# Hedgehog attention and a gated MLP on one core: the first loads change queues, and their order changes

## The chip, the cores and the metric

The kernel runs on one core of one Trainium2 chip. The core has five engines with instruction queues of their own: PE (TensorE, matrix multiplication and transposes, results in PSUM), DVE (VectorE), ACT (ScalarE), POOL (GpSimd) and SP (SyncE, which here only issues transfers). Transfers between main memory and the on-chip memory are moved by 16 DMA engines. A transfer issued by SP or ACT goes through what the profile calls a hardware queue (q1 for SP, q10 for ACT), one issued by POOL through a software queue (q0). In this kernel the transfers that change the number type on the way, fp32 in memory to bf16 on the chip, are issued by POOL; those that SP issues keep the type.

The metric is the device time of one execution in microseconds. The kernel before the change took 287.19 us (median of 11 runs, 286.33 to 287.76).

## The reference

Two layers follow each other. The first is linear attention with learned features (8 batches, 8 heads, 576 tokens, 64 values a head, 128 features; all in fp32):

```python
def phi(x):
    proj = einsum('bhsd,df->bhsf', x, w_phi)
    proj = proj - max(abs(proj), axis=-1, keepdims=True)
    return concatenate([exp(proj), exp(-proj)], axis=-1)
q_p, k_p = phi(q), phi(k)
kv  = einsum('bhsf,bhsd->bhfd', k_p, v)
z   = sum(k_p, axis=2)
num = einsum('bhsf,bhfd->bhsd', q_p, kv)
den = einsum('bhsf,bhf->bhs', q_p, z)[..., None] + 1e-06
return num / den
```

The second takes the result as x, 8 batches of 576 tokens by 512:

```python
h = maximum(x @ w_in, 0.0)                 # w_in 512 x 1024
u, v = h[..., :512], h[..., 512:]
v_n = (v - mean(v)) / sqrt(var(v) + 1e-06) # over the last axis
v_s = einsum('ts,bsd->btd', w_spatial, v_n) + b_spatial[None, :, None]
return (u * v_s) @ w_out
```

What matters here: the sums kv and z of a head run over all 576 tokens of it, so no output of a head can be formed before all its keys and values were seen.

## The kernel before, in words

**Tiles.** 576 tokens are four blocks of 128 and a tail of 64. Two heads of one batch, four blocks each, make one *pair unit*: 128 partitions (tokens) and eight slots (two heads by four blocks). The tails of all eight heads of two batches make one *tail unit*: 64 + 64 partitions and eight slots, one a head. Two batches make a group g; its tail unit is shared by its eight pair units, since each head's sum needs its tail tokens too. The units are worked through in the order: unit 0 and 1 (batch 0, heads 0 to 3), unit 2 (the tail of batches 0 and 1, the "shared tail"), units 3 and 4 (batch 0, heads 4 to 7), units 5 to 8 (batch 1), unit 9 (the tail of batches 2 and 3), and so on: 36 units.

**What a unit does.** `a_transpose` (lines 243 to 256) turns k and q on PE, and DVE (at first) copies them out. `a_keys` multiplies by `w_phi`, DVE takes the maxima of the absolute values (line 273), ACT the two exponentials kf of the key features (line 276). `a_scale` (lines 293 to 309) lets ACT form em, exp of minus and plus the maximum (line 296), and then POOL multiplies v by em: vs for a pair unit (lines 301 and 303), vst for a tail unit (`tail_scale`, lines 311 to 318). So the keys' maximum is not subtracted, but multiplied into v. `a_queries` and `a_max_t` find and turn the queries' maxima (POOL makes mhl from unit 5 on, lines 290 and 291), `a_qfeat` forms the query features qf. `a_kv` (lines 363 to 379) sums kv on PE: for each head and sign four matrix products over the blocks (line 373) and one over the tail's rows (line 375), into one PSUM bank. Every pair unit of a batch therefore waits for that batch's half of vst. `a_num` multiplies by qf and divides.

**The second layer.** When a batch's four pair units are through, its matrix products go into a list of tasks (`b_tasks`), from which the steps fill PE. POOL normalises v there (vn, line 459) and makes the means and roots (lines 451 to 455).

**Steps.** The main loop runs steps i = 0, 1, ...; in step i come the keys of unit i with their scaling, its queries, the transposes of unit i + 1, and the later stages of earlier units, with lags. After step i the transfers of `io[i]` are issued, as the lines `at(i, ...)` at the end of the kernel say (lines 675 to 707): loads of later batches, weights, and for batch 0 and 1 some filling.

**Order on an engine.** The framework orders instructions of an engine by its own simulation, but what is wrapped in `pin` (line 60) stays behind everything already written for its engine. All loads are pinned, and so are fills, casts of the head and `tail_scale`. An engine works its queue in order: while POOL waits for a transfer, what stands behind it waits too, the transfers that it would issue among them.

**The head.** SP loads the first two k and q quarters of batch 0 as fp32 (`first`), which are then cast, two by DVE and two by POOL (lines 162 and 179). POOL issues the rest in this order (lines 174 to 184): the tails of k and q (two loads each, one a batch), k and q of heads 4 and 5, the first half of v; then its two casts; the tail of v (two loads), k and q of heads 6 and 7, the second half of v. The constants `vnt`, rows of the identity that carry the spatial bias through the tail's product, are filled by ACT for even groups before the steps and by POOL for odd ones after step 1 (`fill_vnt`, line 165). The buffers `v_f` for v exist twice; `k_tl`, `q_tl` and `v_tl` for the tails once.

Of the kernel before, what the change touches and what calls it, by code (L numbers as in the profile page):

```python
# [8 lines left out]
FP32 = mybir.dt.float32  # L9
# [7 lines left out]
def kernel(  # L17
# [15 lines left out]
    nc = tc.nc  # L33

    B, H, S, D = q.shape
    F = w_phi.shape[1]
    DM = moe_w_in.shape[0]
    DFF = moe_w_in.shape[1]
    HALF = DFF // 2
    P = 128  # L40
    KC = DM // P
    NP = H // 2
    NB = 4
    T0 = NB * P
    TL = S - T0
# [5 lines left out]
    ld = ctx.enter_context(tc.tile_pool(name="loads", bufs=2))  # L51
# [8 lines left out]
    def pin(start):  # L60
        return lambda *a, **kw: tc.keep_in_program_order(start(*a, **kw))  # L61

    def main_ap(t, b, h0=0, n=H):
        return bass.AP(tensor=t.tensor, offset=t.offset + (b * H + h0) * S * D,
                       ap=[[NB * D, P], [S * D, n], [1, NB * D]])

    def tail_ap(t, b):
        return bass.AP(tensor=t.tensor, offset=t.offset + b * H * S * D + T0 * D,
                       ap=[[D, TL], [S * D, H], [1, D]])

    st = {}
    gs = {}

    XB = 2

    def alloc(b):
        st[b] = dict(
            q=[None, None], k=[None, None],
            v=ld.tile([P, H * NB, D], FP32, tag="v_f", name="v_f"),
        )  # L80

    def alloc_tail(g):
        gs[g] = dict(
            q=ld.tile([P, H, D], BF16, tag="q_tl", name="q_tl", bufs=1),
            k=ld.tile([P, H, D], BF16, tag="k_tl", name="k_tl", bufs=1),
            v=ld.tile([P, H, D], FP32, tag="v_tl", name="v_tl", bufs=1),
        )

    def half_tile(x, b, y):
        if b not in st:  # L90
            alloc(b)
        if st[b][x][y] is None:
            n = f"{x}_bf{(2 * b + y) % 4}"
            st[b][x][y] = ld.tile([P, 4, NB * D], BF16, tag=n, name=n, bufs=1)
        return st[b][x][y]

    def load(x, b, y, h0=0, n=4):
        t = half_tile(x, b, y)
        pin(nc.gpsimd.dma_start)(out=t[:, h0:h0 + n], in_=main_ap(q if x == "q" else k, b, 4 * y + h0, n))

    def load_v(b, y=None, eng=nc.sync):
        if b not in st:
            alloc(b)
        h0, n = (0, H) if y is None else (4 * y, 4)
        pin(eng.dma_start)(
            out=st[b]["v"][:, h0 * NB:(h0 + n) * NB, :].rearrange("p (h c) d -> p h (c d)", h=n),
            in_=main_ap(v, b, h0, n))

    def load_tail(x, g, veng=nc.sync):
        if g not in gs:  # L110
            alloc_tail(g)
        t, eng = dict(q=(q, nc.gpsimd), k=(k, nc.gpsimd), v=(v, veng))[x]
        for i in range(2):
            pin(eng.dma_start)(out=gs[g][x][i * TL:(i + 1) * TL], in_=tail_ap(t, 2 * g + i))
# [12 lines left out]
    first = {}  # L127
    for h0 in (0, 2):
        for x, t in (("k", k), ("q", q)):
            first[x, h0] = s2.tile([P, 2, NB * D], FP32, tag="ob", name="first", bufs=6)  # L130
            pin(nc.sync.dma_start)(out=first[x, h0], in_=main_ap(t, 0, h0, 2))
    ident = cpool.tile([P, P], BF16)
    make_identity(nc, ident)
    zero = cpool.tile([P, 1], BF16)
# [11 lines left out]
    for i in range(NM):  # L146
        for tiles, name in ((mhl, "mhl"), (mT, "mT")):
            t = cpool.tile([P, P], BF16, name=f"{name}{i}")
# [16 lines left out]
    def fill_vnt(i, copy):  # L165
        for bl, row in ((0, TL), (1, 0)):
            pin(copy)(out=vnt[i][:, bl, :], in_=ident[:, row:row + 1].to_broadcast([P, HALF]))

    pin(nc.scalar.copy)(out=vst[0].rearrange("p b s h d -> p (b s h d)"), in_=zero.to_broadcast([P, 4 * H * DA]))
    for y in range(2):  # L170
        r = slice(y * D, (y + 1) * D)
        pin(nc.scalar.copy)(out=wphi2[r, y * F:(y + 1) * F], in_=wphi_f[r, :])
    fill_vnt(0, nc.scalar.copy)
    load_tail("k", 0)
    load_tail("q", 0)
    load("k", 0, 1, 0, 2)
    load("q", 0, 1, 0, 2)
    load_v(0, 0, nc.gpsimd)
    for x in ("k", "q"):
        pin(nc.gpsimd.tensor_copy)(out=half_tile(x, 0, 0)[:, 2:4], in_=first[x, 2])  # L180
    load_tail("v", 0, nc.gpsimd)
    load("k", 0, 1, 2, 2)
    load("q", 0, 1, 2, 2)
    load_v(0, 1, nc.gpsimd)

    w_in_bf = cpool.tile([P, KC, DFF], BF16)
    w_out_bf = cpool.tile([P, KC, DM], BF16)
    wsp = s2.tile([P, NB, T0], BF16, tag="vn", name="wsp", bufs=2)
    wspr = cpool.tile([P, NB, TL], BF16)
# [5 lines left out]
    rows = moe_w_spatial[0:T0, :].rearrange("(p c) s -> p c s", c=NB)  # L195
    cols = moe_w_in.rearrange("(kc p) f -> p kc f", p=P)
# [472 lines left out]
    AT, AB, XP = 5, 6, 3  # L669
    io = {}  # L670

    def at(i, f, *a):
        io.setdefault(i, []).append(lambda: f(*a))

    at(0, load, "k", 1, 0)
    at(0, load, "q", 1, 0)
    at(1, fill_vnt, 1, nc.gpsimd.tensor_copy)
    at(1, load, "k", 1, 1)
    at(1, load, "q", 1, 1)
    at(1, load_v, 1)  # L680
    at(2, load_weight, w_in_bf[:, :, HALF:DFF], cols[:, :, HALF:DFF])
    at(4, load_weight, wsp, rows[:, :, 0:T0])
    at(4, load_weight, wspr, rows[:, :, T0:S])
    at(4, load_weight, wspt, moe_w_spatial[T0:S, :])
    at(5, tail_scale, 0, 1)
    at(5, load_weight, w_in_bf[:, :, 0:HALF], cols[:, :, 0:HALF])
    at(8, load_weight, w_out_bf, moe_w_out.rearrange("(kc p) f -> p kc f", p=P))
    for u in units:
        i = u["i"]
        if not u["pair"] and u["g"] > 0:  # L690
            early = 1 if u["g"] > 1 else 0
            at(i - AT - early, load_tail, "k", u["g"])
            for x in ("q", "v"):
                at(i - AT + 1 - early, load_tail, x, u["g"])
        if u["pair"] and u["b"] >= XB:
            if u["pj"] == 0:
                for n, (x, y) in enumerate((("k", 0), ("q", 0), ("k", 1), ("q", 1))):
                    at((3, 3, 5, 6)[n] if u["b"] == XB else i - AB + n, load, x, u["b"], y)
                for y in range(2):
                    at(i - AB + 1 + 2 * y, load_v, u["b"], y)  # L700
            for x in ("k", "q"):
                at(i - XP, cross, x, u)
# [41 lines left out]
```

## Time and profile before

| | |
|---|---|
| median of 11 runs | 287.19 us |
| the profiled execution, whole | 287.0 us |
| its span, first to last instruction | 285.0 us |
| mean granted clock of PE | 0.985 |
| PE busy | 258.6 us, 91% |
| DVE busy | 230.3 us, 81% |
| ACT busy | 220.5 us, 77% |
| POOL busy | 203.6 us, 71% |
| read from main memory, written | 32.85 MB, 9.44 MB |

Times in the profile are counted from the span's start. A row of the timeline gives start, duration, engine, line, operation, the tile written and the tile read, and in brackets how long the engine had been idle before it and what released it. A row of the waits gives who waited for whom, the sum, how often, and the longest. The chain is followed back from the last instruction, at each step to what released it; a DMA in it begins when it was issued. Line 61 is the pin helper, so pinned instructions all carry that line and are told apart by their tiles. A transfer "lands" when its semaphore says so; its piece counts are those of the written side. Issuing a transfer takes POOL 0.5 to 0.9 us, which its rows show as work of its own; on SP it is a row of SPq.

### The profile page before, as it was taken

The page shows a single profiled execution, that of the slowest core. Times are in us where ns is not written, and L with a number is a line of the kernel's source. Part 1 is how long each engine was busy: PE and PEld are TensorE (multiplying, and loading weights), DVE is VectorE, ACT ScalarE, POOL GpSimd, SP SyncE. Part 2 cuts the span into 40 slices and gives each one's busy share as a digit, 9 for nine tenths or more (in the row PEclk, how much of TensorE's full clock was granted, in tenths as well). Part 3 has the DMA queues.
Part 4 walks back from the last instruction along what each step waited for, and adds up shares of the span by engine and source line. Part 5 has one row for each costly group of instructions (what it writes and reads, how often), then busy time and mean ns, then how long its engine had stood idle before and what let it go on. Part 6 is the DMA issues. An engine that isn't in the chain of part 4 may idle for free.

```text
span 285.0 us, 8175 instructions
## 1 busy us (share of the span) xinstructions
PE 258.6 (91%) x3042; PEld 172.4 (60%) x3042; DVE 230.3 (81%) x576; ACT 220.5 (77%) x501; POOL 203.6 (71%) x366
## 2 busy tenths in 40 slices
PE   3751988989899899999999999999999999999993
PEld 2531876666666576667666676666765765654441
DVE  6970998986799997998889989997889897566441
ACT  6690898997699997899889987899789977723601
POOL 8679999999987895699958984789558832420710
PEclk9996899999999999999999999999999999999998
DMA  9989999999967999989997999999756301120205
GB/s 188 285 143 132 149 115 134 218 157 205 179 96 125 157 226 199 160 221 194 191 127 109 243 235 145 207 192 229 96 120 132 80 8 44 68 76 37 112 3 184
DMA packets 83420, 42.17 MB, mean 148 GB/s; under 512 B 51122, under 2 KB 78450, under 8 KB 83380
## 3 DMA queue, kind: packets, MB, share of 16 engines
q1 hardware_dynamic: 55796, 29.12, 51.5%
q0 software_dynamic: 27424, 12.46, 36.8%
q8 instruction: 24, 0.39, 0.6%
q14 instruction: 16, 0.13, 0.2%
q10 hardware_dynamic: 160, 0.07, 0.1%
HBM read 32.85 MB, written 9.44 MB: 148 GB/s over the span
## 4 chain that ended last, share of the span: by engine, by line
PE 59%; POOL 20%; DVE 6%; DMA 5%; ACT 4%; issue 3%; POOLq 0%; ACTq 0%; DVEq 0%
PE ps L518 9%; PE pv L442 9%; PE po L543 9%; PE ps L261 6%; PE pu L497 6%; POOL vs L301 5%; PE pv L373 4%; DMA v_f<-in_v_dram 4%; PE pn L393 4%; POOL vst L61 3%; PE pq L339 3%; PE ps L519 2%; ACT kf L276 2%; POOL vn L459 2%; DVE stats L445 2%
## 5 line engine op out<-in xcount | busy, mean ns | idle before, releaser
L276 ACT ACTIVATE kf<-ps 128x512 bf16<-128x512 f32 x144 | 76.2, 636 | 8.3 <-DVE mk L273 8.0
L301 POOL TENSOR_TENSOR vs<-v_f,em 128x512 bf16<-128x512 f32 x64 | 65.4, 1041 | 19.6 <-ACT em L296 18.0
L360 ACT ACTIVATE qf<-pq 128x512 bf16<-128x512 f32 x128 | 66.8, 622 | 15.6 <-PE pq L339 8.5
L273 DVE TENSOR_REDUCE mk<-ps 128x4 f32<-128x512 f32 x72 | 47.6, 677 | 0.8
L287 DVE TENSOR_REDUCE mq<-ps 128x4 f32<-128x512 f32 x62 | 39.8, 681 | 2.5 <-PE ps L261 2.2
L518 PE MATMUL ps<-w_spT,vn 128*128 128x512 bf16 x128 | 33.7, 379 | 1.4 <-POOL vn L459 1.4
L521 DVE TENSOR_TENSOR uT<-ps,uT 128x512 bf16<-128x512 f32 x32 | 22.0, 687 | 14.4 <-PE ps L519 14.3
L445 DVE BATCH_NORM_STATS2 stats<-vr 128x6 f32<-128x512 bf16 (+1 forms) x40 | 26.7, 683 | 7.5 <-ACT vr L444 7.1
L543 PE MATMUL po<-w_out_bf,uT 128*128 128x512 bf16 x128 | 32.4, 379 | 0.0
L497 PE MATMUL pu<-xT,w_in_bf 128*128 128x512 bf16 x128 | 32.1, 379 | 0.0
L442 PE MATMUL pv<-w_in_bf,xT 128*128 128x512 bf16 x128 | 31.5, 379 | 0.1
L444 ACT ACTIVATE vr<-pv 128x512 bf16<-128x512 f32 (+1 forms) x40 | 23.5, 616 | 7.3 <-PE pv L442 5.9
L373 PEld LDWEIGHTS <-kf 128*128 128x128 bf16 x512 | 22.1, 98 | 11.3 <-issue 10.3
L375 PE MATMUL pv<-vst,kf 128*128 128x66 bf16 x128 | 21.5, 193 | 7.0 <-POOL vst L61 7.0
L373 PE MATMUL pv<-vs,kf 128*128 128x66 bf16 x512 | 24.8, 195 | 2.9 <-POOL vs L303 1.6
L384 DVE TENSOR_TENSOR x<-pn,rc 128x256 bf16<-128x256 f32 x64 | 24.9, 418 | 0.3
L459 POOL TENSOR_SCALAR vn<-vr,rs 128x512 bf16<-128x512 bf16 x32 | 24.3, 766 | 1.1
L393 PEld LDWEIGHTS <-qf 128*128 128x128 bf16 x512 | 20.4, 98 | 6.8 <-issue 0.8
L499 ACT ACTIVATE uT<-pu 128x512 bf16<-128x512 f32 x32 | 19.7, 641 | 4.9 <-PE pu L497 3.2
L546 ACT COPY ob<-po 128x512 f32<-128x512 f32 x18 | 11.0, 613 | 15.1 <-PE po L543 8.6
L393 PE MATMUL pn<-kv,qf 128*128 128x66 bf16 x512 | 21.9, 194 | 0.3 <-ACT qf L360 0.3
L61 POOL TENSOR_TENSOR vst<-v_tl,em 64x512 bf16<-64x512 f32 x16 | 16.4, 1040 | 5.3 <-ACT em L296 4.9
(134 smaller groups left out, 569.7 us busy)
## 6 DMA issues: line engine op xcount, KB each, us to landing
out_dram<-ob SPq DMA_DIRECT2D x32, 256.0 KB, 2.6
v_f<-in_v_dram SPq DMA_DIRECT2D x12, 512.0 KB, 7.1
k_bf<-in_k_dram POOLq DMA_DIRECT2D x14, 256.0 KB, 5.4
q_bf<-in_q_dram POOLq DMA_DIRECT2D x14, 256.0 KB, 5.2
qt<-qT_b SPq DMA_DIRECT2D x24, 64.0 KB, 4.8
v_f<-in_v_dram SPq DMA_DIRECT2D x1, 1024.0 KB, 8.8
v_f<-in_v_dram POOLq DMA_DIRECT2D x2, 512.0 KB, 8.9
w_in_bf<-in_moe_w_in_dram POOLq DMA_DIRECT2D x2, 512.0 KB, 6.4
```

The costliest lines, as they stand in the source:

```text
L273: nc.vector.tensor_reduce(out=u["mk"][:, hs], in_=pk, axis=AX.X, op=ALU.max, apply_absolute_value=True)
L276: nc.scalar.activation(out=u["kf"][:, s, hs, :], in_=pk, func=AF.Exp, bias=0.0, scale=sc)
L287: nc.vector.tensor_reduce(out=mq[:, 4 * half:4 * half + 4], in_=pq, axis=AX.X, op=ALU.max, apply_absolute_value=True)
L301: nc.gpsimd.tensor_tensor(out=vs[:, s, :, 0:D], in0=st[u["b"]]["v"][:, pj * H:(pj + 1) * H, :], in1=em[:, s, :].unsqueeze(2).to_broadcast( ...
L360: nc.scalar.activation(out=qf[:, s], in_=pq, func=AF.Exp, bias=0.0, scale=sc)
L373: nc.tensor.matmul(out=pv[:, hh, s, :], lhsT=u["kf"][:, s, 4 * hh + c, :], rhs=u["vs"][:, s, 4 * hh + c, :], start=(c == 0), stop=False)
L393: nc.tensor.matmul(out=pn[:, pos, :], lhsT=u["qf"][hh][:, s, pos, :], rhs=d["kv"][:, 2 * u["pj"] + hh, s, :], start=(s == 0), stop=(s == 1))
L442: nc.tensor.matmul(out=pv[r], lhsT=lhs(kc), rhs=w_in_bf[:, kc, HALF:DFF], start=(kc == 0), stop=(kc == KC - 1))
L445: nc.vector.bn_stats(out=stats[r], in_=dst[r])
L497: nc.tensor.matmul(out=pu, lhsT=w_in_bf[:, kc, dc * P:(dc + 1) * P], rhs=d["xT"][:, kc, :], start=(kc == 0), stop=(kc == KC - 1))
L518: nc.tensor.matmul(out=ps, lhsT=d["vn"][:, sp, cs], rhs=w_spT[:, sp, 0:T0], start=(sp == 0), stop=False)
L543: nc.tensor.matmul(out=po[r], lhsT=lhs(dc), rhs=w_out_bf[:, dc, :], start=(dc == 0), stop=(dc == KC - 1))
```

## The change

The first tails, fp32, and batch 0's v come through SP's queue, after the four `first` loads and in this order: tail of k (two loads), tail of q (two), first half of v, tail of v (two), second half of v. The k and q tails land in a buffer `tails` of the kind of `v_f`, and POOL casts them to `k_tl` and `q_tl`. All four `vnt` fills are made by POOL ahead of its other work; the ones of ACT and the later ones of POOL are gone. POOL's two casts of `first` then come before its loads of heads 4 and 5, and the loads of heads 6 and 7 come behind the tail casts.

In the steps, v of batch 1 is issued on SP after step 1 as before; k and q of batch 1 move from steps 0 and 1 to 2 and 3, behind the scaling of the tail in step 2; the second half of `w_in` from 2 to 4; two of the three spatial loads from 4 to 5, behind the scaling of the tail's second batch; the first half of `w_in` from 5 to 6; and the k and q loads of batch 2 by one step each.

```diff
+    alloc_tail(0)
+    tails = ld.tile([P, H * NB, D], FP32, tag="v_f", name="tails")
+    for n, t in enumerate((k, q)):
+        for i in range(2):
+            pin(nc.sync.dma_start)(out=tails[i * TL:(i + 1) * TL, n * H:(n + 1) * H, :], in_=tail_ap(t, i))
+    load_v(0, 0)
+    load_tail("v", 0)
+    load_v(0, 1)
     ident = cpool.tile([P, P], BF16)
     make_identity(nc, ident)
...
-    fill_vnt(0, nc.scalar.copy)
-    load_tail("k", 0)
-    load_tail("q", 0)
+    for i in range(2):
+        fill_vnt(i, nc.gpsimd.tensor_copy)
+    for x in ("k", "q"):
+        pin(nc.gpsimd.tensor_copy)(out=half_tile(x, 0, 0)[:, 2:4], in_=first[x, 2])
     load("k", 0, 1, 0, 2)
     load("q", 0, 1, 0, 2)
-    load_v(0, 0, nc.gpsimd)
-    for x in ("k", "q"):
-        pin(nc.gpsimd.tensor_copy)(out=half_tile(x, 0, 0)[:, 2:4], in_=first[x, 2])
-    load_tail("v", 0, nc.gpsimd)
+    for n, x in enumerate(("k", "q")):
+        pin(nc.gpsimd.tensor_copy)(out=gs[0][x], in_=tails[:, n * H:(n + 1) * H, :])
     load("k", 0, 1, 2, 2)
     load("q", 0, 1, 2, 2)
-    load_v(0, 1, nc.gpsimd)
...
-    at(0, load, "k", 1, 0)
-    at(0, load, "q", 1, 0)
-    at(1, fill_vnt, 1, nc.gpsimd.tensor_copy)
-    at(1, load, "k", 1, 1)
-    at(1, load, "q", 1, 1)
     at(1, load_v, 1)
-    at(2, load_weight, w_in_bf[:, :, HALF:DFF], cols[:, :, HALF:DFF])
-    at(4, load_weight, wsp, rows[:, :, 0:T0])
-    at(4, load_weight, wspr, rows[:, :, T0:S])
+    at(2, load, "k", 1, 0)
+    at(2, load, "q", 1, 0)
+    at(3, load, "k", 1, 1)
+    at(3, load, "q", 1, 1)
+    at(4, load_weight, w_in_bf[:, :, HALF:DFF], cols[:, :, HALF:DFF])
     at(4, load_weight, wspt, moe_w_spatial[T0:S, :])
     at(5, tail_scale, 0, 1)
-    at(5, load_weight, w_in_bf[:, :, 0:HALF], cols[:, :, 0:HALF])
+    at(5, load_weight, wsp, rows[:, :, 0:T0])
+    at(5, load_weight, wspr, rows[:, :, T0:S])
+    at(6, load_weight, w_in_bf[:, :, 0:HALF], cols[:, :, 0:HALF])
...
-                    at((3, 3, 5, 6)[n] if u["b"] == XB else i - AB + n, load, x, u["b"], y)
+                    at((4, 4, 6, 7)[n] if u["b"] == XB else i - AB + n, load, x, u["b"], y)
```

## The prediction

> **What bounds the kernel now.** I read the page's busy shares first, then the chain in order of time, the waits of the first 30 us, the rows of POOL, and sums over stretches.
>
> ```profile
> span 285.0 us, 8175 instructions
> PE 258.6 (91%) x3042; PEld 172.4 (60%) x3042; DVE 230.3 (81%) x576; ACT 220.5 (77%) x501; POOL 203.6 (71%) x366
> PE 59%; POOL 20%; DVE 6%; DMA 5%; ACT 4%; issue 3%; POOLq 0%; ACTq 0%; DVEq 0%
> ```
>
> Over the whole span PE is the bound, but POOL holds a fifth of the chain. Where, the busy time by stretch tells (start:end, length, then PE, PEld, DVE, ACT, POOL, the granted clock, DMA):
>
> ```profile
> 18.00:24.00 6.00, 1.56 (x23) 1.40 (x23) 1.82 (x5) 3.20 (x9) 5.99 (x10) 0.98 0.74 97
> 24.00:30.00 6.00, 2.90 (x29) 2.40 (x29) 1.74 (x5) 1.47 (x3) 5.97 (x10) 0.50 0.92 114
> 28.00:75.00 47.00, 42.96 (x603) 32.90 (x600) 40.15 (x110) 42.26 (x99) 44.13 (x80) 0.97 1.18 168
> 75.00:285.00 210.00, 203.01 (x2330) 130.48 (x2326) 172.60 (x417) 161.55 (x367) 137.04 (x251) 1.00 0.81 138
> ```
>
> From 18 to 30 us PE, DVE and ACT are all mostly idle and POOL is full; up to 75 POOL is the fullest (44.13 of 47); from 75 on PE is (203.01 of 210, 97%), so time won before 75 reaches the end. The waits of the first 30 us name the stall:
>
> ```profile
> DVE kv L378 <- PE pv L375: 7.7, 1, 7.7
> PE pv L375 <- POOL vst L61: 7.0, 1, 7.0
> POOL vs L301 <- ACT em L296: 3.5, 1, 3.5
> POOL v_f L61 <- DMA q_tl<-in_q_dram: 0.9, 1, 0.9
> ```
>
> PE stood 7.0 us, until 27.10, for the scaled shared tail. POOL's own 3.5 us before its first scaling is put down to em, which had ended at 9.62; the chain shows the true releaser, the first v, issued at 5.94 and landed at 16.15, and behind it POOL's queue:
>
> ```profile
> 5.94 10.21 DMA v_f<-in_v_dram
> ...
> 16.29 2.04 POOL vs L301 x2
> ...
> 24.81 2.25 POOL vst L61 x3
> 27.10 0.21 PE pv L375
> ```
>
> In POOL's rows there lie between 16.29 and 24.81: two unit scalings (2.2 each), four cast loads (0.80, 0.76, 0.80, 0.75) and two fills (1.17).
>
> **The change part by part.** *Issues taken off POOL.* Tail k 1.69, tail q 1.39, v 0.79 and 0.78, tail v 1.40: 6.05 us. *Put on POOL:* two fills that ACT did, four in all, 4 x 0.59 = 2.3 us, and two tail casts.
>
> ```profile
> 6.71 0.64 POOL L61 CAST k_bf<-first 128x512 bf16<-128x512 f32 x1
> 7.74 0.61 POOL L61 CAST q_bf<-first 128x512 bf16<-128x512 f32 x1 [0.38 <-DMA first<-in_q_dram]
> 22.12 1.17 POOL L61 COPY vnt<-ident 128x512 bf16<-128x512 bf16 x2
> ```
>
> The tail casts have the size of these casts: 2 x 0.63 = 1.25 us. The fills need only the identity (ready 1.29), so they run to 3.7 under the wait for the first k and q; that cover is 1.9 us, and without it they would cost 2.3. ACT's 1.14 us of fills go, at no gain: its next work waited for DVE's first maxima anyway.
>
> The Trainium skill (GPSIMD Engine Reference, Engine selection) sends elementwise work to VectorE, GpSimd being about twice as slow for two inputs and near line rate for one. Here the same cast took 0.36 and 0.48 on DVE against 0.64 and 0.61, so even with one input it is slower. By the rule the tail casts would go to DVE, POOL would be 1.25 us shorter and the sum 281.7; but DVE was busy 6.00 of 6.00 us from 12 to 18.
>
> *When things land on SP's queue.* Two rows set the pace: one microsecond in which this queue worked nearly alone, on 1 KB pieces, and three in which it moved only the 256-byte pieces of the tail v.
>
> ```profile
> q1 hardware_dynamic: 306, 0.29, 90.2%
> ...
> q1 hardware_dynamic: 410, 0.10, 26.8%
> ```
>
> The first gives 0.29 MB per us, so a 256 KB load each 0.9 us. The second: 26.8% of 16 engines over 3.0 us, by 410 pieces, is 31 ns a piece. The first k lands at 3.77 as before (0.72 + 3.05); the others, no longer beside POOL's loads and batch 1's v, at 4.7, 5.6 and 6.5, where the issue-to-landing times were 3.0 to 5.4 (last landing 7.7). So POOL's casts end at 6.2 and 7.1, and its first two k and q loads (0.73 + 0.72) at 8.6. The four tails are 2048 pieces: 2048 x 31 ns / 16 = 4.0 us behind 6.5, so k is whole at 8.5 and q at 10.5. What competes are the two POOL loads just issued, 512 pieces of 60 ns: at most 1.9 us more. So the tail q lands between 10.5 and 12.4; I take the middle, 11.4. Issuing is no limit: four issues of 0.66 (the 64-partition tail v on SP) from 2.73. A ninth load in flight waits for the landing of the first, as SP's v did (0.5 us for wphi); those are down by 4.8.
>
> *The POOL queue then.* Tail k cast to 9.2, tail q cast 11.4 to 12.0, the other k and q loads (1.48) to 13.5. These loads wait behind the casts now and are issued 2.3 us later than before (9.67 and 10.37, landings 17.81 and 18.21); with the SP queue shorter by batch 1's v I estimate 5.5 rather than 8 us, so they land at about 17.5 to 18.3, and unit 4's transposes (18.67) still find them. v's first half needs 1.8 us more on SP's ring and lands at 13.2. First scaling at **13.5** (12.6 to 14.5) instead of 16.29: 2.8 us won (1.8 to 3.7). Its second half lands by 18.9, needed at 21.7; the tail v by 17.1, needed at 17.9.
>
> Unit 0, unit 1 and the tail now follow directly: 13.5 + 2.2 + 2.2 + 2.3 = **20.2** instead of 27.1. PE's stall shrinks from 7.0 us to at most 0.3. Of the clock: it was 0.86 at 23 to 24 and 0.50 in 24 to 30, after 4 us of idle PE, and PE's 16 matmuls of line 393 took 0.97 there against 0.66 later. With no such idle time this goes too; I count nothing, since DVE sets that stretch (busy from 28.18 to 46 almost without a gap).
>
> *What is late next.* POOL. All of its work to 75 is still to be done, only without the 1.2 us of fills that stood in the queue and the 0.4 us wait for em at 31.4: from the first scaling on it is the same list in another order. So at the end of its full stretch POOL is ahead by 2.8 + 1.2 + 0.4 = 4.4 us, not 6.9.
>
> *Loads moved behind the tail's scaling.* Batch 1's first k and q (0.80 + 0.76) move past unit 1 and the tail: issued 20.2 and 21.0 (before 18.43, 19.22). With 4.8 us to land, as before, q is there at 25.8; PE transposed it at 31.51, so in the new flow at 31.51 - 6.9 = 24.6. A new wait of 1.2 us, behind which stand the tail's features and unit 5's keys; DVE copied this transpose 1 us after PE made it, so some 0.2 is left. The bounds: 0, and 21.0 + 12.5 - 24.6 = 8.9 from the slowest landing of a q load in the first 60 us; I stay near the low end, since the load beside it is nearest to the rows at 19 and 24 us. Batch 1's second halves come at 24 and land by 29, needed past 34. Batch 1's v waits on SP for the two tail casts, whose buffer it takes: issued at 12 instead of 3.98, landing 8.8 us later at 20.8, needed when POOL scales unit 5 (39.14 before, some 35 now). Behind it on SP stand the tail v and v of later batches, issued from 42 on. Of the weights, the second half of w_in leaves POOL at about 27 (needed 49.3 before), the spatial ones at about 38 (needed 57.6), the first half at about 43 (needed 64.0); each has 7 us or more of cover over the 6 to 7.4 that such loads took, and nothing is counted. Batch 2's k and q halves are issued one step later, which costs POOL nothing in sum.
>
> The sum: 4.4 - 0.2 = 4.2 us. The profiled execution took 287.0 (2.0 around the span), 0.2 under the median of 287.19; 287.0 - 4.2 = 282.8, and **283.0** as a median. With the landings at their bounds POOL's gain is 3.4 to 5.3, so 281.7 to 283.9 for this case alone.
>
> **The rivals.** *More is won* (about 280.2): POOL's fullness up to 75 is partly work that nobody waits for, loads and masks, and the gain is PE's and DVE's: the 7.0 us stall. For it: in 28 to 75 PE's largest single wait for POOL is 0.8. Against: the chain is POOL's nearly without a break from 36 to 74.
>
> *Less is won* (about 285.4): the middle of the head is set by transfers. In 42 to 54 us loads took 7.4 to 12.9 us, and the spatial weights, issued at 34 before, are moved towards that crowd. If the crowd ends 1.6 rather than 4.2 us earlier, that is what remains.
>
> *Slower* (about 288.2): the load of batch 1's first q becomes the stall that the tail was. The place is unit 5's transposes; before they ran at 31.51 and the q load had landed at 24.0. It decides if that load, issued at 21.0, needs over 11.5 us (31.51 + 1.0 of slack in DVE's copy - 21.0); in the crowd 12.5 were seen, which makes 33.5 and costs 1.0 us. Against: batch 1's v, the only big load beside it, ends at about 20.8.
>
> *No change* (287.2): the order in which PE meets the tail is traded for one with the same idle time elsewhere. Only the 7.7 us of idle DVE turning up again would show it.
>
> **How the numbers follow.** Main case 0.50, more 0.23, less 0.14, no change 0.04, slower 0.09. Some 0.2% (0.6 us) is what a measurement of this kernel can tell from no change; the first three are faster by more: 0.87. The range goes from 279.4, where PE's stall and DVE's 7.7 us are won whole, to 286.5, the poor end of "less"; above it lie no change and slower, 0.13. The main case's own range is 281.7 to 283.9.
>
> **What would show it.** Right: POOL's first scaling at 12.6 to 14.5; PE's wait for vst under 1 us, kv at about 20.5; the granted clock near 1.00 from 24 to 30; the vn that ended POOL's stretch (73.9) at about 69.7. Wrong: the tail q landing after 12.4; a PE wait of over 2 us at unit 5's transposes near 25; spatial weights or w_in ending waits near 50; or POOL ahead at 45 us and no longer at 74.

## The result, and the profile after

The changed kernel took 284.77 us (median of 12 runs, 282.98 to 286.29) against 287.34 for the kernel before (47 runs). The ratio is 0.9906, with a 95% interval of 0.989 to 0.9922: 2.7 us faster by the ratio, 2.6 by the two medians. The forecast was 283.0, in a range of 279.4 to 286.5. The profiled execution of the changed kernel took 283.99, 0.8 under its median, so its stretches are read against the 287.0 of before with that much of doubt.

Line numbers behind the head are 6 higher now (`a_scale`'s product L301 is L307, em L296 is L302, the tail's product on PE L375 is L381). First the page: span, busy shares, the chain by engine.

```profile
span 282.2 us, 8175 instructions
PE 260.6 (92%) x3042; PEld 173.0 (61%) x3042; DVE 231.2 (82%) x576; ACT 219.7 (78%) x499; POOL 200.6 (71%) x362
PE 61%; POOL 13%; DVE 8%; DMA 6%; ACT 6%; issue 3%; SPq 0%; POOLq 0%; ACTq 0%; DVEq 0%
```

POOL's part of the chain fell from 20% to 13%. Busy time by stretch (start:end, length, PE, PEld, DVE, ACT, POOL, the granted clock, DMA), with the two long stretches chosen as long as those of before:

```profile
18.00:24.00 6.00, 5.92 (x66) 4.98 (x65) 4.60 (x15) 5.56 (x13) 4.18 (x7) 0.72 0.92 165
24.00:30.00 6.00, 5.11 (x99) 4.48 (x98) 6.00 (x18) 5.48 (x14) 5.52 (x9) 1.00 0.81 102
25.00:72.00 47.00, 41.62 (x565) 30.71 (x562) 38.04 (x106) 40.82 (x97) 44.29 (x79) 0.96 1.26 164
72.00:282.00 210.00, 203.16 (x2334) 130.60 (x2330) 172.76 (x417) 161.71 (x368) 137.21 (x252) 1.00 0.82 141
```

From 18 to 30 us PE is busy for 11.0 us instead of 4.5, and the engine that stands still there is now POOL (4.18 and 5.52 of 6). The last 210 us are what they were, and so is the stretch ahead of them, with POOL the fullest (44.29 of 47). So 2.8 us of the head went, and behind it the sums stayed. Of the waits of the first 32 us, the three that matter for what follows:

```profile
POOL k_bf L61 <- DMA first<-in_k_dram: 2.6, 1, 2.6
POOL vs L307 <- ACT em L302: 2.5, 3, 1.8
PE pt L260 <- DMA k_bf<-in_k_dram: 2.4, 1, 2.4
```

PE's 7.0 us for vst and DVE's 7.7 us for PE are gone. The first line is what is left, behind the fills, of POOL's wait for its first k. The other two the prediction did not have: PE's wait for the k of unit 3, and POOL's wait for the em of units 3 and 4. POOL's rows (start, duration) show the latter:

```profile
6.70 0.61 POOL L61 CAST k_bf<-first 128x512 bf16<-128x512 f32 x1 [2.59 <-DMA first<-in_k_dram]
7.82 0.61 POOL L61 CAST q_bf<-first 128x512 bf16<-128x512 f32 x1 [0.51 <-DMA first<-in_q_dram]
...
12.96 2.04 POOL L307 TENSOR_TENSOR vs<-v_f,em 128x512 bf16<-128x512 f32 x2 [0.21 <-ACT em L302]
...
17.26 2.03 POOL L61 TENSOR_TENSOR vst<-v_tl,em 64x512 bf16<-64x512 f32 x2
...
22.75 2.04 POOL L307 TENSOR_TENSOR vs<-v_f,em 128x512 bf16<-128x512 f32 x2 [1.82 <-ACT em L302]
...
26.91 2.04 POOL L307 TENSOR_TENSOR vs<-v_f,em 128x512 bf16<-128x512 f32 x2 [0.48 <-ACT em L302]
28.91 0.20 POOL L309 CAST vs<-em 128x32 bf16<-128x32 f32 x1
29.05 0.80 POOL L61 DMA_DIRECT2D w_in_bf<-in_moe_w_in_dram  x1
...
31.75 0.82 POOL L61 DMA_DIRECT2D k_bf<-in_k_dram  x1
32.51 0.81 POOL L61 DMA_DIRECT2D q_bf<-in_q_dram  x1
```

The first scaling comes 3.33 us earlier than before (16.29), unit 4's scaling 4.94 earlier (31.85 to 26.91). But POOL stood 1.82 + 0.48 us on the way there, and three loads that stood ahead of unit 4 are behind it now (29.05, 31.75, 32.51). What released unit 3's em is in the chain (a DMA in it runs from its issue to its landing):

```profile
9.34 7.93 DMA q_bf<-in_q_dram
17.32 0.40 PE pt L260 x4
...
20.51 2.07 ACT kf L282 x4
22.57 0.18 ACT em L302 x2
```

The q of heads 4 and 5, issued at 9.34, landed at 17.28; before it had landed at 13.70.

One cost of the new head stays hidden here. While POOL makes the four fills (1.36 to 4.10 us), two small operations of DVE take longer, and DVE's first cast of k, and with it PE's first work, comes 0.8 us later. The rows before the change, and then those after it:

```profile
2.00 0.10 DVE L61 TENSOR_TENSOR sel<-ident 128x8 bf16<-128x8 bf16 x1
2.14 0.73 DVE L61 TENSOR_SCALAR sel<-sel 128x1024 bf16<-128x1024 bf16 x1
...
3.90 0.36 DVE L61 CAST k_bf<-first 128x512 bf16<-128x512 f32 x1
```

```profile
2.00 0.54 DVE L61 TENSOR_TENSOR sel<-ident 128x8 bf16<-128x8 bf16 x1
2.58 1.06 DVE L61 TENSOR_SCALAR sel<-sel 128x1024 bf16<-128x1024 bf16 x1
...
4.66 0.36 DVE L61 CAST k_bf<-first 128x512 bf16<-128x512 f32 x1
```

It cost nothing at the first scaling, because v landed only at 12.81, long after unit 0's em (9.97; 9.62 before).

### The profile page after: what moved, and what is told of

The parts are those of the page before. It is cut to its first block, busy times and chain, and to the rows that moved or that the text cites. A ratio compares the mean times of both kernels' runs of the same rounds, so it can differ in the third digit from the quotient of the medians.

```text
span 282.2 us, 8175 instructions
## 1 busy us (share of the span) xinstructions
PE 260.6 (92%) x3042; PEld 173.0 (61%) x3042; DVE 231.2 (82%) x576; ACT 219.7 (78%) x499; POOL 200.6 (71%) x362
## 4 chain that ended last, share of the span: by engine, by line
PE 61%; POOL 13%; DVE 8%; DMA 6%; ACT 6%; issue 3%; SPq 0%; POOLq 0%; ACTq 0%; DVEq 0%
PE pv L448 10%; PE ps L524 9%; PE po L549 9%; PE ps L267 6%; PE pu L503 6%; PE pv L379 4%; ACT kf L282 3%; PE pn L399 3%; PE pq L345 3%; DMA q_bf<-in_q_dram 3%; POOL vs L307 2%; POOL vst L61 2%; PE ps L525 2%; DVE stats L451 2%; DMA first<-in_q_dram 2%
## 5 line engine op out<-in xcount | busy, mean ns | idle before, releaser
L307 POOL TENSOR_TENSOR vs<-v_f,em 128x512 bf16<-128x512 f32 x64 | 65.4, 1043 | 18.1 <-ACT em L302 16.6
L366 ACT ACTIVATE qf<-pq 128x512 bf16<-128x512 f32 x128 | 66.6, 620 | 10.5 <-PE pq L345 8.5
L448 PE MATMUL pv<-w_in_bf,xT 128*128 128x512 bf16 x128 | 32.2, 385 | 0.1
L381 PE MATMUL pv<-vst,kf 128*128 128x66 bf16 x128 | 21.3, 192 | 0.0
```

The costliest lines, as they stand in the source:

```text
L307: nc.gpsimd.tensor_tensor(out=vs[:, s, :, 0:D], in0=st[u["b"]]["v"][:, pj * H:(pj + 1) * H, :], in1=em[:, s, :].unsqueeze(2).to_broadcast( ...
L366: nc.scalar.activation(out=qf[:, s], in_=pq, func=AF.Exp, bias=0.0, scale=sc)
L448: nc.tensor.matmul(out=pv[r], lhsT=lhs(kc), rhs=w_in_bf[:, kc, HALF:DFF], start=(kc == 0), stop=(kc == KC - 1))
```

## The experiments

All ratios are to the kernel before; their 95% intervals stand with each run below (0.989 to 0.9922 for the change itself). The other columns are from one profiled execution each: the start of the first scaling and of unit 4's, the end of the fourth vn, POOL's time between those two, and from that vn to the end of the span.

| run | ratio | first scaling | unit 4's scaling | fourth vn ends | between | vn to end |
|---|---|---|---|---|---|---|
| before | 1 | 16.29 | 31.85 | 73.97 | 42.1 | 211.0 |
| after | 0.9906 | 12.96 | 26.91 | 71.12 | 44.2 | 211.1 |
| head_only | 0.9883 | 13.63 | 29.10 | 71.14 | 42.0 | 211.2 |
| steps_only | 1.0067 | 15.51 | 30.42 | 74.63 | 44.2 | 211.7 |
| pool_extra | 0.9967 | 12.66 | 25.29 | 71.71 | 46.4 | 211.1 |
| loads_first | 0.9912 | 13.89 | 27.39 | 71.60 | 44.2 | 212.6 |
| head_loads_first | 0.9988 | 15.05 | 31.93 | 73.95 | 42.0 | 211.2 |
| k1_early | 0.9928 | 12.44 | 26.37 | 70.66 | 44.3 | 212.5 |
| casts_dve | 1.0050 | 15.26 | 30.89 | 75.12 | 44.2 | 211.3 |
| masks_dve | 0.9874 | 12.91 | 27.36 | 69.59 | 42.2 | 212.9 |
| head_masks | 0.9939 | 13.17 | 29.83 | 70.65 | 40.8 | 213.6 |
| fill_gaps | 0.9856 | 12.83 | 26.95 | 69.06 | 42.1 | 213.4 |
| fill_gaps_masks | 0.9871 | 13.68 | 27.70 | 68.72 | 41.0 | 213.8 |
| fill_gaps_tail | 0.9878 | 12.50 | 26.77 | 68.96 | 42.2 | 212.0 |

**Which part carries the gain.** Two kernels take the change apart. One has the new head with the step order of before:

```diff
+    at(0, load, "k", 1, 0)
+    at(0, load, "q", 1, 0)
+    at(1, load, "k", 1, 1)
+    at(1, load, "q", 1, 1)
...
-    at(2, load, "k", 1, 0)
...
-    at(4, load_weight, w_in_bf[:, :, HALF:DFF], cols[:, :, HALF:DFF])
+    at(2, load_weight, w_in_bf[:, :, HALF:DFF], cols[:, :, HALF:DFF])
...
-                    at((4, 4, 6, 7)[n] if u["b"] == XB else i - AB + n, load, x, u["b"], y)
+                    at((3, 3, 5, 6)[n] if u["b"] == XB else i - AB + n, load, x, u["b"], y)
```

> The changed kernel with the steps' loads put back where they were: batch 1's k and q after steps 0 and 1, the second half of w_in after 2, the spatial weights after 4, the first half of w_in after 5, batch 2's k and q a step earlier. Theory (POOL's list sets the time to 75 us; with loads between the first scalings POOL works through the 1.8 us in which it now waits for unit 3's em): POOL's vst ends at about 22.7 instead of 19.5, PE waits for it, and yet the time is 282.0 to 283.2, lower than the changed kernel's 284.6. Rival (moving the loads behind the tail's scaling is what brought the gain): PE's wait for vst is back, and the time is 285.8 to 287.2.

The other, steps_only, is the old head with the new step order, the same lines the other way round.

> The kernel before with only the steps' loads moved as in the change; the head is as before, the constant fill after step 1 as well. Theory (POOL's list sets the time, and no work is taken off it): vst ends at about 24.1 instead of 27.1, PE's stall is 3 us shorter, and the time is 286.3 to 287.3, no change or 0.4 us less, the wait for unit 4's em. Rival (PE's stall is the gain): 284.0 to 284.9.

Measured: head_only 0.9883 [0.9862, 0.9905], steps_only 1.0067 [1.004, 1.0094]. The new head alone wins all that the whole change wins; its interval overlaps with that of the whole. Its time, 284.25, lies above the theory's range and below the rival's, so neither named it. PE's wait for vst came back at only 0.8 us, and POOL still stood 0.18 us for unit 3's em and 1.30 for unit 4's:

```profile
POOL vs L307 <- ACT em L302: 1.5, 2, 1.3
```

The moves of loads alone cost 1.9 us; neither expectation allowed for a loss. Two of the waits of steps_only in its first 32 us:

```profile
PE pv L375 <- POOL vst L61: 5.2, 1, 5.2
...
POOL vs L301 <- ACT em L296: 2.1, 1, 2.1
```

PE's wait for vst became shorter, by 1.8 us, as the moves are meant to do. But POOL then had nothing to issue ahead of unit 4's em, stood 2.1 us (0.44 before), and issued the loads afterwards. The table says the same of all runs: with the old step order POOL needs 42.0 to 42.1 us from unit 4's scaling to the fourth vn, with the new one 44.2 to 44.3 (in the runs that change neither masks nor fills and fill no gaps). In that stretch it had no wait. In steps_only's profile POOL waits 1.69 us more, its first scaling came 0.78 earlier, and the fourth vn ended 0.66 later; the span is 1.3 longer, and that the rest of the 1.9 us is of the same kind is not shown. On the new head the moves brought unit 4 forward by 2.2 us (29.10 to 26.91) and lengthened the stretch behind it by 2.2.

**Is it POOL's list that counts?** Two more pairs of fills are put into POOL's queue behind unit 4, with nobody waiting for them:

```diff
+    for _ in range(2):
+        at(4, fill_vnt, 1, nc.gpsimd.tensor_copy)
```

> The changed kernel, with the two constant fills of one group made twice more after step 4: four copies of 0.58 us, 2.3 us more on POOL at about 29 us and nothing else. Theory (from unit 4's scaling to 75 us POOL's list of work sets the time): the end moves by 2.0 to 2.5 us, to 286.6 to 287.1. Rival (the gain was PE's stall, and POOL's fullness is work nobody waits for): less than 0.5 us, at most 285.1.

```profile
21.20 2.04 POOL L307 TENSOR_TENSOR vs<-v_f,em 128x512 bf16<-128x512 f32 x2 [0.57 <-ACT em L302]
...
25.29 2.04 POOL L307 TENSOR_TENSOR vs<-v_f,em 128x512 bf16<-128x512 f32 x2 [0.41 <-ACT em L302]
...
28.77 2.29 POOL L61 COPY vnt<-ident 128x512 bf16<-128x512 bf16 x4
```

Measured: 0.9967 [0.9945, 0.9989], 0.0061 or 1.75 us above the changed kernel; with both intervals this is 1.0 to 2.5 us. Of 2.29 us put into POOL's list some three quarters reach the end, and the stretch is 2.2 longer. So POOL's list bounds the time up to the fourth vn; the rival, that its fullness is work that nobody waits for, allowed less than 0.5 us and falls.

The profile of pool_extra shows one thing more. Up to unit 4 it is the code of the changed kernel, and yet POOL's two new waits are 0.57 + 0.41 us in it, not 1.82 + 0.48. The k and q of unit 3 landed earlier (14.20 and 16.08, not 16.24 and 17.28), and PE's granted clock was 1.00 from 18 to 24 us, not 0.72. From the start of q's transposes to the end of unit 3's em it took 5.07 us there and 5.44 in the changed kernel. Unit 3's em came 1.56 us later in the changed kernel, some 1.2 of it by the later landing and some 0.4 on the path behind. So the size of that wait belongs to one execution; what both share is that there is one.

**Can the new wait be taken away?** The k and q loads of heads 4 and 5 are issued behind POOL's casts of `first`; if that is where unit 3's wait comes from, issuing them ahead, as in loads_first, must remove it:

```diff
-    for x in ("k", "q"):
-        pin(nc.gpsimd.tensor_copy)(out=half_tile(x, 0, 0)[:, 2:4], in_=first[x, 2])
...
+    for x in ("k", "q"):
+        pin(nc.gpsimd.tensor_copy)(out=half_tile(x, 0, 0)[:, 2:4], in_=first[x, 2])
```

> The changed kernel, with the k and q loads of heads 4 and 5 issued by POOL ahead of its two casts of the first loads instead of behind them. Theory (the missed term is that these loads were moved behind the casts, landed at 16.24 and 17.28 instead of 12.96 and 13.70, and made POOL wait 1.82 us for unit 3's em and 0.48 for unit 4's): the loads are issued at about 4.2 and land by 13.5, the wait for unit 3's em goes under 0.3 us, and the time falls by 1.6 to 2.3 us against the changed kernel's 284.6, to 282.3 to 283.0. Rival (the head's transfers share one rate, so an earlier k and q means later tails and v): the first scaling moves from 12.96 to 14.5 or later, and the time stays within 0.4 us of 284.6.

Measured: 0.9912 [0.9886, 0.9937], no gain, as the rival had it (though the first scaling moved to 13.89, not to its 14.5). The two halves landed at 9.40 and 10.99 and POOL's wait for unit 3 shrank to under 0.2, so the late loads were its source, but:

```profile
PE pv L381 <- POOL vst L61: 3.0, 1, 3.0
...
POOL vs L307 <- ACT em L302: 1.8, 1, 1.8
```

The two loads of the tail's q now landed at 11.07 and 11.46 (before this edit 9.88 and 10.64) and v's first half at 13.74 (12.81). In the ten profiles whose head issues these loads behind the casts, the last of the tail's q landed at 10.30 to 11.34 and v at 12.06 to 13.54; in the two that issue them ahead, at 11.46 and 12.46, and at 13.74 and 14.90. So the earlier k and q are paid for with later tails and a later v. And PE, with unit 3 early, met the sums kv ahead of unit 4's transposes and stood 3.0 us for vst. So unit 4's em came at 27.40 and POOL's wait had moved one unit on. The same edit on head_only's step order:

> The queue part alone, with the k and q loads of heads 4 and 5 ahead of POOL's casts. Theory (every order in this head ends in a wait of POOL for em, of unit 3 where its k and q are late, of unit 4 where vst holds PE up; the loads put between fill part of it): vst ends at about 23.5, POOL waits some 2 us before unit 4's scaling, and the ratio is 0.988 to 0.993, no better than the queue part alone (0.9883). Rival (unit 3's late k and q were a loss of their own): 1.3 us less, ratio 0.982 to 0.985.

Measured: 0.9988 [0.9968, 1.0008]; both expectations missed. PE waited 6.1 us for vst and POOL 2.9 for unit 4's em, and unit 4 began at 31.93, no earlier than in the kernel before. In k1_early one pair of loads goes back ahead of the tail's scaling:

```diff
-    at(2, load, "k", 1, 0)
-    at(2, load, "q", 1, 0)
+    at(1, load, "k", 1, 0)
+    at(1, load, "q", 1, 0)
```

> The changed kernel with one step of its schedule put back: the first k and q loads of the second batch are issued after step 1 instead of step 2, so POOL issues them ahead of the scalings of the shared tail; they take 1.55 us of its queue. Theory (what sets the end is the moment at which POOL starts unit 4's scaling, and what its list holds from there on): the last shared scaling ends 1.55 us later, near 20.9, but the loads then lie inside POOL's 1.82 us wait for unit 3's em, of which some 0.3 is left; unit 4's scaling starts within 0.4 us of 26.91 and the time is that of the changed kernel, ratio 0.989 to 0.992 to the kernel before. Rival (PE's wait for the scaled tail is what counts): the end moves by the whole 1.55 us, ratio near 0.996.

Measured: 0.9928 [0.9908, 0.9948]. The second product of vst ended 1.05 us later (20.34 for 19.29), and unit 4's scaling began at 26.37, 0.5 earlier, as the theory has it; the time lies just above its range, and the rival's 0.996 is outside the interval. The span grew by 1.0 us although the fourth vn came 0.5 earlier: PE was busy only 3.43 us of 66 to 72, and waited 2.6 us there for vn, which it had reached early. What it lost afterwards stands in PE's rows behind the last vn, first those of the changed kernel, then those of k1_early:

```profile
71.62 0.66 PE L399 MATMUL pn<-kv,qf 128*128 128x66 bf16 x16
72.21 0.70 PE L427 MATMUL pn<-kv,qf_t 128*64 128x66 bf16 x16
```

```profile
71.54 1.09 PE L399 MATMUL pn<-kv,qf 128*128 128x66 bf16 x16
72.56 1.09 PE L427 MATMUL pn<-kv,qf_t 128*64 128x66 bf16 x16
```

The granted clock was 0.50 from 71 to 74 us in k1_early, and 1.00 in the changed kernel. From its first product behind the fourth vn to the next products for query features PE took 4.19 us in k1_early (70.71 to 74.90) and 2.75 in the changed kernel (71.18 to 73.93): 1.44 us more, about what the two differences, 0.5 earlier and 1.0 later, make together. In loads_first the same work took 4.23 us (71.66 to 75.89), with the clock at 0.50 from 73 to 75, and its rest in the last column is 212.6.

**The casts on DVE.** The rule weighed in the prediction (the Trainium skill, GPSIMD Engine Reference, Engine selection) sends elementwise work to VectorE. So:

```diff
-        pin(nc.gpsimd.tensor_copy)(out=gs[0][x], in_=tails[:, n * H:(n + 1) * H, :])
+        pin(nc.vector.tensor_copy)(out=gs[0][x], in_=tails[:, n * H:(n + 1) * H, :])
```

> The changed kernel with the two tail casts made by DVE, as the prediction weighed by the Trainium skill (GPSIMD Engine Reference, Engine selection). Theory (v's landing at 12.81 sets the first scaling, at 12.96, so POOL has nothing to gain there, and the casts meet a DVE that is busy): within 0.6 us of the changed kernel, ratio 0.989 to 0.993. By the page's rule, as weighed in the prediction: 1.25 us off POOL, ratio 0.986.

Measured: 1.005 [1.0027, 1.0072], slower than the kernel before and 4.1 us above the changed one; both expectations missed.

```profile
PE ps L267 <- DVE kT L262: 6.2, 4, 5.4
...
DVE k_tl L61 <- DMA tails<-in_k_dram: 3.8, 1, 3.8
```

The cast itself is shorter on DVE (0.43 us for 0.62). But it stands in DVE's queue where the code puts it, ahead of unit 0's copies kT, and waits there 3.8 us for the tail's k; PE waits 5.4 for those copies, and unit 0's em ends at 15.27 instead of 9.97. On POOL the same casts run at 10.07 and 10.76, with no wait ahead of them. What the rule goes by, the faster engine, holds here; what decided at this place is the wait that the cast brings into a queue worked in order. A version with the casts further back in DVE's queue was not tried, so no run shows that DVE is the wrong engine for them wherever they stand.

**The masks on DVE.** The three instructions that build `wm` (lines 241 to 243), which are worked off four times, go to DVE. These are twelve single instructions and 4.0 us of POOL's list behind unit 4, not the twelve pairs and 4.3 us of the expectation:

```diff
-            pin(nc.gpsimd.tensor_copy)(out=wm[:, j, :], in_=wphi2[:, 0:F])
+            pin(nc.vector.tensor_copy)(out=wm[:, j, :], in_=wphi2[:, 0:F])
...
```

> The changed kernel with the twelve pairs of small operations that build the mask weights wm (some 4.3 us on POOL between 45 and 53 us) made by DVE. Theory (POOL's list sets the time to 75 us; the added fills cost 1.75 of their 2.3 us): POOL reaches its last vn of the head 3 to 4 us earlier, PE had some 2 us of idle time between 44 and 75, and the ratio to the kernel before goes from 0.9906 to 0.982 to 0.987, 282.1 to 283.6 us. Rival (nothing behind 45 us waits for POOL but through the order of its queue): within 0.4 us of the changed kernel, ratio 0.989 to 0.992.

> The queue part alone (the steps' loads where they were, as in the run before, which gave 0.9883) with the mask weights made by DVE. Theory: both gains add, ratio 0.977 to 0.985, 280.7 to 283.0 us, lower than both kernels. Rival (PE's order after the late vst sets the time): 0.987 to 0.990.

Measured: 0.9874 [0.9831, 0.9917] on the changed kernel, which is not told apart from the changed kernel itself and holds parts of both expected ranges; 0.9939 [0.9917, 0.9962] on head_only, worse there than without the edit, and outside both. POOL's waits from 20 to 75 us in masks_dve:

```profile
POOL vs L307 <- ACT em L302: 2.8, 2, 1.9
POOL var L458 <- DVE mv_t L452: 2.6, 1, 2.6
```

A shorter list of POOL runs into DVE's statistics of the second layer (`mv_t`): of the 4.0 us taken off POOL's list 2.6 are waited away, 3.4 in head_masks. The wait is a new one; the list is not the only bound here, only the nearest.

**Loads put into the waits.** If POOL's list counts and POOL stands 2.3 us ahead of unit 4, then what is behind unit 4 and needs no em belongs into that gap:

```diff
-    at(3, load, "k", 1, 1)
+    at(2, load_weight, w_in_bf[:, :, HALF:DFF], cols[:, :, HALF:DFF])
+    at(2, load, "k", 1, 1)
...
-    at(4, load_weight, w_in_bf[:, :, HALF:DFF], cols[:, :, HALF:DFF])
...
-                    at((4, 4, 6, 7)[n] if u["b"] == XB else i - AB + n, load, x, u["b"], y)
+                    at((3, 3, 6, 7)[n] if u["b"] == XB else i - AB + n, load, x, u["b"], y)
```

> The changed kernel with three sets of loads moved up into POOL's two waits for em (1.82 us ahead of unit 3's scaling, 0.48 ahead of unit 4's): the second half of w_in from step 4 to step 2, the second batch's second k load to step 2, the third batch's first k and q loads from step 4 to step 3. Theory (the waits are idle time of the engine that sets the end, and the moved loads cost nothing inside them): unit 4's scaling starts near 27.3 instead of 26.91, POOL's stretch from there to the last normalised v falls from 44.2 to about 41.8, and the end comes some 2.0 us earlier: ratio 0.981 to 0.986, near 282.6. Rival (the loads make unit 4's k and q land later, or the waits come back further on): 0.989 to 0.992, as the changed kernel.

Measured: 0.9856 [0.983, 0.9883], 283.11 us: faster than both kernels, and the lowest ratio of the study, though its interval overlaps with those of head_only, masks_dve and the two runs below. POOL's rows:

```profile
20.79 0.76 POOL L61 DMA_DIRECT2D w_in_bf<-in_moe_w_in_dram  x1
21.52 0.77 POOL L61 DMA_DIRECT2D k_bf<-in_k_dram  x1
22.52 2.04 POOL L307 TENSOR_TENSOR vs<-v_f,em 128x512 bf16<-128x512 f32 x2 [0.22 <-ACT em L302]
...
26.95 2.08 POOL L307 TENSOR_TENSOR vs<-v_f,em 128x512 bf16<-128x512 f32 x2
```

Half of w_in and the second batch's second k lie in what was the wait of 1.82 us, and the third batch's first k and q stand between units 3 and 4. Unit 4 begins where it did, and the stretch behind is 42.1 again. So the theory held, and the fourth vn ended 2.06 us earlier. The time followed by 1.4 (0.0050 of 287.3; 0.5 to 2.3 with both intervals) to 1.7 us (medians). In the profiled execution, one at the upper end of its runs (284.49), the end did not follow at all, and PE's waits from 30 to 80 us and its busy time from 48 to 54 say where it stuck:

```profile
PE pt L260 <- DMA q_tl<-in_q_dram: 2.8, 1, 2.8
```

```profile
48.00:54.00 6.00, 3.14 (x22) 2.65 (x24) 2.51 (x8) 2.82 (x7) 5.63 (x13) 0.75 1.31 171
```

The second tail's q took 12.1 us to land; PE, 2 us ahead of its old time, found it missing. Two runs went after the remainder. The first joins the masks on DVE to it:

> The same three moves of loads, and the weights with the maximum's mask on DVE instead of POOL. Theory (POOL's list sets the end and the two gains add): some 0.9 us below the run with the moved loads alone, as the same edit won alone, ratio 0.978 to 0.984. Rival (with POOL earlier it waits for DVE's masks instead, as it waited 3.4 us in the run that joined them to the old step order): not below the run with the moved loads alone.

Measured: 0.9871 [0.9847, 0.9895], not below fill_gaps, as the rival had it; POOL's wait for DVE is 3.5 us now:

```profile
POOL var L458 <- DVE mv_t L452: 3.5, 1, 3.5
```

The second issues the spatial weights behind that q:

```diff
-    at(5, load_weight, wsp, rows[:, :, 0:T0])
-    at(5, load_weight, wspr, rows[:, :, T0:S])
     at(6, load_weight, w_in_bf[:, :, 0:HALF], cols[:, :, 0:HALF])
+    at(6, load_weight, wsp, rows[:, :, 0:T0])
+    at(6, load_weight, wspr, rows[:, :, T0:S])
```

> The run with the loads moved into POOL's gaps, and one move more: the spatial weights' two loads (576 KB, 1.58 us of POOL's queue) are issued in step 6 behind the first half of w_in instead of in step 5 ahead of the second shared tail's q. There POOL's fourth normalised v ended 2.06 us earlier than in the changed kernel, yet PE waited 2.8 us near 50 for that q, which landed 12.1 us after its issue, and the steady part began no earlier. Theory (that landing took back the profiled run's gain): q of the second tail is issued near 36.2 and lands before 48.5, PE's 2.8 us wait is gone, the end follows the fourth normalised v by about 211 us again: profiled span 280 to 281, ratio 0.978 to 0.984. Rival (PE, DVE and POOL are all near their limits ahead of 76 us, and the next wait is a few tenths behind): 0.984 to 0.988, not told apart from the run without the move.

Measured: 0.9878 [0.9853, 0.9903], not told apart from fill_gaps. The q landed 5.4 us after its issue and PE's 2.8 us are gone, but from 30 to 80 us PE now waits for the weights that were moved:

```profile
PE pt L216 <- DMA wsp<-in_moe_w_spatial_dram: 2.0, 1, 2.0
```

Its profiled span is 281.0, at the end of the theory's range, but its six runs (283.04 to 284.23) are not lower than those of fill_gaps. As far as these runs show, POOL's list, PE's operands from memory and DVE's statistics come within about 2 us of each other up to 76 us: in five of the six runs in which the fourth vn ended ahead of 71 us the rest took 212.5 to 213.8 us, not 211.1, and in the sixth, fill_gaps_tail, 212.0. In k1_early the low clock behind vn accounts for it. In fill_gaps, masks_dve, head_masks and fill_gaps_masks the clock is 1.00 from 66 to 78 us and PE is busy for at least 11.8 of these 12 us (11.28 in the changed kernel), so there it is PE's own list that is left over.

## Why the prediction was right, and where it was not

The direction was right and the time in its range, 1.8 us above the point. The range was wide: the main case's own, 281.7 to 283.9, was missed by 0.9, and 284.77 lies nearer to the 285.4 of "less". (With the 0.2 for the q load taken off and the 0.2 to the median put on, as in the point, the main case's bounds of 3.4 and 5.3 come to 284.0 and 282.1; it is missed by that too.) Step by step:

- *The stall of PE and DVE goes, and the gain is what POOL is ahead by, not 6.9 us.* Right. PE's wait for vst is gone, the second product of vst ended at 19.29 (20.2 was said for the whole tail, 26.86 before), the first kv at 21.84 (20.5 said), and the vn that closes POOL's stretch moved by 2.85 us, to 71.12 (69.7 said), while the span moved by 2.8. pool_extra shows that this is POOL's list and not a coincidence; "more is won", whose argument was that nobody waits for that list, fell with it.
- *Landings.* The later k and q of `first` were said to come at 5.6 and 6.5, because nothing of POOL's is beside them now. They came at 6.64 and 7.76, before the change at 6.57 and 7.68: the loads of POOL beside them did not set them. What does is open; SP's own loads of the tails lie beside them now. The tail's q was said to land between 10.5 and 12.4 and landed at 9.88 and 10.64; v 13.2, landed 12.81. The errors cancel: first scaling 13.5 said, 12.96 measured, inside its 12.6 to 14.5. That term was 3.33 us, not 2.8; in the nine profiles with this head and POOL's casts the first scaling began at 12.44 to 13.68, so half a microsecond either way is luck.
- *Fills and the em wait at 31.4.* 1.17 and 0.44 us, as said. With these the end of POOL's stretch should gain 3.33 + 1.17 + 0.44 = 4.94 us. The cover of the fills was not quite free: beside them DVE's first cast came 0.8 us later, and no run here shows that this cost time.
- *The step that failed:* "from the first scaling on it is the same list in another order". The list is the same, but it has two new waits in it, 1.82 + 0.48 = 2.30 us, for em of units 3 and 4. 4.94 - 2.30 = 2.64, against 2.85 measured at the vn. Without its waits the list from the first scaling to the fourth vn is the same to 0.2 us: 56.07 before (fills taken off), 55.86 after, 56.03 in head_only. In the place where the moved loads stood POOL is idle now, and they are issued later at full price. Unit 4's scaling itself came 4.94 us earlier only because the loads that went behind it (2.35 us of the list) are about as long as the new waits; that this equals the sum above is chance. In head_only the waits are 1.48 us and the first scaling is 0.67 later, which comes to the same vn (71.14). steps_only shows the waits without the new head, and fill_gaps gives 1.4 us back by filling them.
- Behind it is a landing that was worked out but not followed through. The k and q loads of heads 4 and 5 were put "done" at 8.6; they were issued at 8.38 to 10.06, and landed at 16.24 and 17.28, 3.3 and 3.6 us later than before. Only the loads of heads 6 and 7 were priced against their user (unit 4's transposes), and at an estimated 5.5 us to land; they took 7.5 and 8.4. Unit 3 comes first, and it waited: PE 2.4 us for its k.
- *The clock.* "Near 1.00 from 24 to 30": 1.00. But the slow stretch did not go, it moved: 0.72 from 18 to 24, behind PE's idle time ahead of 17.3, and 0.77 from 42 to 48 (behind 1.4 us of waiting for mhl). The prediction put the clock at nothing. It can matter: PE began unit 3's transposes of k and q at 14.25 and 16.13 in pool_extra and at 14.15 and 16.08 in k1_early, but unit 3's em ended at 21.20 and 22.02; from 12 to 18 and 18 to 24 the clock was 1.00 and 1.00 in the one, 0.84 and 0.88 in the other. No run changes the clock alone.
- *Slower* (unit 5's q load as the new stall): nothing of it. That q was said to land at 25.8 and landed at 25.38, and PE had no wait of over 0.2 us for it. The 0.2 us counted for it were not needed.
- *Less is won* was the rival nearest in number (285.4), but not in mechanism: no transfer ended a PE wait of over 0.2 us in the changed kernel from 30 to 80 us. The crowd appears only once POOL is faster still, in fill_gaps and fill_gaps_tail.

## What to carry to other kernels

When a queue in order is the bound, moving loads behind urgent work is a gain only if that work can start; else the queue idles ahead of it and pays for the loads afterwards. So look for the wait that will open in front of the promoted work, and leave in it whatever needs no input. When a load is moved, follow it to its first user, not to the one that the trace of before shows near it. And before a cast or copy goes to the faster engine, look at what stands behind it in that engine's queue when the transfer lands: on a queue in order the wait of the cast is passed on to all behind it (3.8 us on DVE here, none on POOL).

## What the runs showed of the hardware

- The last two of the first loads landed at 6.57 and 7.68, and 6.41 and 7.51 us, in the two profiles of the old head, with POOL's loads beside them; at 6.15 to 7.28 and 7.27 to 8.51 in the ten of the new head without; at 6.71 and 7.52, and 7.47 and 8.42, in the two where two of POOL's loads were put beside them again. Taking POOL's loads away did not bring them forward, and executions of one head differ by 1.1 to 1.2 us.
- Landings in the crowd differ between executions of the same code: with the head and the first steps alike, PE started unit 3's transposes of k at 16.29 (after), 15.03 (masks_dve), 14.60 (fill_gaps), 14.25 (pool_extra) and 14.15 (k1_early). Unit 4's scaling began anywhere from 25.29 to 27.36 in these five, not in the order of the landings: it was earliest where the granted clock was 1.00 from 18 to 24 us (pool_extra) and latest where it was lowest (0.64, masks_dve). A single profile places it to about 1 us only; the length of POOL's stretch behind it varied by 0.1.
- At a granted clock of 0.50 PE's 16 matmuls of line 399 took 1.09 us, at 1.00 0.66. Low stretches lay behind idle time of PE: 0.50 in 24 to 30 before, 0.72 in 18 to 24 after, 0.75 in 48 to 54 in fill_gaps. But not every idle time had one: in casts_dve PE stood 5.4 us until 11.51, and the clock was 1.00 from 6 to 18 us.
- Beside POOL's four fills two operations of DVE took 0.54 and 1.06 us instead of 0.10 and 0.73, in all twelve profiles of the new head and in neither of the old one. The last of the fills, which ran beside the longer of the two, took 1.06 us; the three ahead of it, and the same fill elsewhere, 0.6.
